# A new order of second-layer matmuls, and D parts made beside them, in a kernel of gated linear attention and four-expert layers

## Chip, cores, metric

One core of a Trainium2 chip. The metric is the device time of one execution, in microseconds (us), lower is better. Executions of one kernel agree within some 0.3%; all runs quoted are marked fast on record.

## The reference, cut

```python
# attention: B=4, H=8, S=768, D=48, state per head
for t in range(S):
    state = alpha[:, :, t, :, None] * state + k[:, :, t] (x) v[:, :, t]
    y[:, :, t] = q[:, :, t] @ state
x = y as (3072, 384)
# four experts, all used: w1 is (4, 384, 1024), w2 is (4, 1024, 384)
p = domain_probs / (domain_probs.sum(-1, keepdims=True) + 1e-9)
for e in range(4):
    out += p[:, e:e+1] * (maximum(x @ w1[e], 0) @ w2[e])
```

## The kernel before

The 3072 rows are 24 blocks of 128, in groups: 0 has two blocks, 1 to 5 have four each, 6 has two. For each group and expert a first layer makes eight hidden tiles (128 features x up to 512 rows), and a second layer multiplies them with w2. From group 2 on the operands of the second layer are in three parts: H (top), L (rest), D (a small correction of the two). H and L products share one sum per block, D has another. There are 16 second layers of full groups (96 matmuls each) and four of group 6 (48). Attention for later groups runs in between.

The first layer makes H on ScalarE, L on VectorE, then half of D at once; the other half goes on a list:

```python
def hidden_parts(x, parts):
    top, low, dif = parts
    nc.scalar.activation(out=top, in_=x, func=ACT.Relu, scale=TRIM)
    yield
    nc.vector.scalar_tensor_tensor(out=low, in0=x, scalar=0.0, in1=top.bitcast(F32),
                                   op0=ALU.max, op1=ALU.subtract)
    n = x.shape[-1]
    at = n // 2 if n == NT else 0
    if at:
        make_dif(*(part[:, :at] for part in parts))
    later.append([part[:, at:] for part in parts])
```

The second layer takes two blocks per call, all their H and L and then all their D. It allots its sums at the start of the call, from the same four buffers (tag "g") that the first layer's sums use:

```python
sums = [[ps.tile([P, DM], F32, name=f"ops{j}", tag="g", bufs=4)
         for j in range(2 if halves_ else 1)] for _ in slots]
kinds = [((0, 1), range(FCH - 2)), ((0, 1), range(FCH - 2, FCH)), ((2,), range(FCH))]
...
    if later and n % 4 == 3:
        make_dif(*later.popleft())
    ... nc.tensor.matmul(sums[i][part // 2], lhsT=h[:, part], rhs=w, ...)
    if part >= 1 and fc == FCH - 1:
        add_up(gi, e, slots[i], part // 2, ...)     # mostly one VectorE operation
```

The last second layer before a new group also splits that group's input (`split_x`, tile xT), in steps at 0, 52, 62 and 72% of the layer.

## Time and profile before

| | before |
|---|---|
| time, 3 runs | 1073.79 us (1073.01 to 1075.13) |
| span in the profile | 1071.6 us |
| TensorE busy | 98% |
| VectorE busy | 72%, 775.2 us |
| second-layer matmuls waiting for add-ups | 4.3 us, four times |

In the profile's lines PE is TensorE, PEld its weight loads, DVE VectorE, ACT ScalarE and POOL GpSimd. An instruction has its line of code, engine, output<-inputs, shapes and count; a wait has its total in us, how often it came, and the longest. The granted clock is the share of the full TensorE clock that the profile shows, as a mean over the span. The chain is the work that ended last, followed back to the start. Busy TensorE isn't the same as TensorE at full pace, so I also read distances from one matmul's start to the next. The prediction below shows the lines.

### The profile page before, as it was taken

The numbers are of one execution on the slowest core, as the hardware profiler recorded it, in microseconds if no ns is written. First come the engines' busy times: TensorE is split into PE (matmuls) and PEld (weight loads), VectorE is DVE, ScalarE is ACT, GpSimd is POOL, SyncE is SP. The second block draws the span as 40 slices with busy tenths as digits, with TensorE's granted clock in tenths as the row PEclk, the third lists the DMA queues.
The fourth block names the chain that finished last, engine by engine and source line by source line (L and its number), as shares of the span: only waits on it lengthen the run. The fifth ranks groups of instructions, "written<-read, shape, count | busy, mean of one in ns | idle before, by whom it ended". The sixth has DMA issues, their size and how long they took to land.

```text
span 1071.6 us, 21614 instructions
## 1 busy us (share of the span) xinstructions
PE 1048.1 (98%) x8460; PEld 899.1 (84%) x8460; DVE 775.2 (72%) x1711; ACT 566.7 (53%) x1202; POOL 32.7 (3%) x71
## 2 busy tenths in 40 slices
PE   8899999999999999999999999999999999999998
PEld 8777777676776798898898898898889889898988
DVE  5488776656566978778877777986787866666565
ACT  5687866575656554536546445555464543323232
POOL 2010000000000100000000000000000000000000
PEclk9999999999999999999999999999999999999999
DMA  8597699687696967758759558586594543544540
GB/s 123 156 330 216 230 328 368 238 328 241 236 309 209 402 216 274 281 160 312 268 170 359 204 187 337 186 281 234 158 358 173 221 192 147 207 177 178 187 181 31
DMA packets 158838, 251.67 MB, mean 235 GB/s; under 512 B 120112, under 2 KB 135344, under 8 KB 136208
## 3 DMA queue, kind: packets, MB, share of 16 engines
q1 hardware_dynamic: 149600, 208.82, 57.1%
q0 software_dynamic: 5760, 41.29, 9.8%
q8 instruction: 67, 1.10, 0.4%
q10 hardware_dynamic: 3376, 0.17, 0.3%
q14 instruction: 35, 0.29, 0.1%
HBM read 207.79 MB, written 42.47 MB: 234 GB/s over the span
## 4 chain that ended last, share of the span: by engine, by line
PE 83%; DVE 8%; ACT 6%; issue 2%; DMA 1%; SPq 0%; DVEq 0%; ACTq 0%
PE ops L624 25%; PE one L540 21%; PE ops L628 10%; PE two L540 10%; PE sc L334 6%; PE yps L428 3%; PE tp L266 3%; PE one L532 2%; ACT qb L308 2%; PE far L389 1%; PE sps L463 1%; DVE near L344 1%; DVE t L553 1%; DVE hT L580 1%; DVE hT L590 1%
## 5 line engine op out<-in xcount | busy, mean ns | idle before, releaser
L624 PE MATMUL ops<-w,hT 128*128 128x384 f32 x1728 | 318.0, 339 | 4.4 <-DVE acc L658 4.3
L624 PEld LDWEIGHTS ops<-w,hT 128*128 128x128 f32 x1728 | 299.1, 188 | 9.9 <-DVE acc L658 5.6
L540 PE MATMUL one<-xT,w 128*128 128x512 f32 x960 | 253.8, 400 | 2.6 <-DVE xT L248 1.1
L540 PEld LDWEIGHTS one<-xT,w 128*128 128x128 f32 x960 | 176.3, 188 | 41.8 <-DVE QT L315 1.6
L551 ACT ACTIVATE t<-one 128x512 f32<-128x512 f32 (+1 forms) x192 | 106.3, 554 | 153.6 <-PE one L540 148.5
L308 ACT COPY qb<-QT 64x256 f32<-64x256 f32 x336 | 136.4, 406 | 77.0 <-DVE QT L289 44.1
L578 ACT ACTIVATE hT<-t 128x512 fp32r<-128x512 f32 (+1 forms) x160 | 94.3, 589 | 123.6 <-DVE t L553 122.9
L580 DVE SCALAR_TENSOR_TENSOR hT<-t,hT 128x512 fp32r<-128x512 f32 (+1 forms) x160 | 102.2, 638 | 55.7 <-ACT hT L578 53.6
L540 PE MATMUL two<-xT,w 128*128 128x512 f32 x480 | 136.7, 393 | 0.0
L628 PE MATMUL ops<-hT 128*128 128x384 f32 x384 | 133.4, 491 | 0.0
L553 DVE TENSOR_TENSOR t<-t,two 128x512 f32<-128x512 f32 (+1 forms) x160 | 100.8, 630 | 41.9 <-ACT t L551 21.4
L590 DVE SCALAR_TENSOR_TENSOR hT<-hT 128x256 fp32r<-128x256 f32 x288 | 111.9, 422 | 4.4
L540 PEld LDWEIGHTS two<-xT,w 128*128 128x128 f32 x480 | 90.6, 189 | 20.0
L628 PEld LDWEIGHTS ops<-hT 128*128 128x128 f32 x384 | 69.5, 190 | 40.1 <-issue 0.4
L315 DVE TENSOR_TENSOR QT<-QT,dec 128x256 f32<-128x256 f32 x144 | 60.8, 422 | 38.2 <-ACT qb L308 37.5
L344 DVE COPY_PREDICATED near<-masks,sc 128x256 f32<-128x256 uint8 x144 | 77.0, 535 | 15.5 <-PE sc L334 12.8
L334 PEld LDWEIGHTS sc<-qb,KT 128*64 128x64 f32 x2304 | 72.7, 138 | 9.7 <-issue 5.6
L334 PE MATMUL sc<-qb,KT 128*64 128x64 f32 x2304 | 77.2, 223 | 2.6 <-ACT qb L308 2.6
L658 DVE SCALAR_TENSOR_TENSOR acc<-ops,p_all,acc 128x384 f32<-128x384 f32 x82 | 49.5, 614 | 33.9 <-PE ops L624 14.5
L326 ACT COPY KT<-KT 128x256 f32<-128x256 f32 x144 | 59.9, 416 | 3.2
L327 DVE TENSOR_TENSOR KT<-KT,dec 128x256 f32<-128x256 f32 x144 | 60.3, 419 | 0.0
L558 DVE TENSOR_TENSOR hT<-t,two 128x512 f32<-128x512 f32 x32 | 22.0, 688 | 35.6 <-ACT t L551 23.0
(88 smaller groups left out, 970.7 us busy)
## 6 DMA issues: line engine op xcount, KB each, us to landing
w<-kept SPq DMA_DIRECT2D x144, 1152.0 KB
kept<-w POOLq DMA_DIRECT2D x32, 1152.0 KB, 7.4
hT<-in_moe_w_dram SPq DMA_DIRECT2D x32, 384.0 KB
w<-in_moe_w_dram SPq DMA_DIRECT2D x48, 128.0 KB
ra<-in_alpha_dram SPq DMA_DIRECT2D x23, 192.0 KB
rk<-in_k_dram SPq DMA_DIRECT2D x23, 192.0 KB
rq<-in_q_dram SPq DMA_DIRECT2D x23, 192.0 KB
out_dram<-acc POOLq DMA_DIRECT2D x18, 192.0 KB, 6.6
```

The source lines that it names most:

```text
L308: nc.scalar.copy(out=qb[rows, :, i, :].rearrange("p a (b r) -> p a b r", r=m), in_=qv[rows])
L315: nc.vector.tensor_mul(qv, qv, spread(dv[:, :, :, 0], m))
L334: nc.tensor.matmul(out[HALF * s:HALF * (s + 1), 2 * p:2 * p + 2, :], lhsT=KTs[li][:, p, HALF * s:HALF * (s + 1)], rhs=qbs[li][:, p, :, QUA ...
L344: nc.vector.copy_predicated(near.rearrange("p a (b two r) -> p a b two r", two=2, r=m)[:, :, :, 1, :], mk.unsqueeze(1).broadcast_to([P, H, ...
L540: nc.tensor.matmul(out, lhsT=w[:, part, kc], rhs=x_part(gi, part, kc), start=(part == terms[0] and kc == 0), stop=(part == terms[-1] and k ...
L551: nc.scalar.activation(out=t, in_=one, func=ACT.Copy, scale=FINE)
L553: nc.vector.tensor_add(t, t, two)
L578: nc.scalar.activation(out=top, in_=x, func=ACT.Relu, scale=TRIM)
L580: nc.vector.scalar_tensor_tensor(out=low, in0=x, scalar=0.0, in1=top.bitcast(F32), op0=ALU.max, op1=ALU.subtract)
L590: nc.vector.scalar_tensor_tensor(out=dif, in0=top.bitcast(F32), scalar=1 / 4096.0, in1=low.bitcast(F32), op0=ALU.mult, op1=ALU.subtract)
L624: nc.tensor.matmul(sums[i][part // 2], lhsT=h[:, part], rhs=w, start=(fc == 0 and part != 1), stop=(fc == FCH - 1 and part != 0))
L628: nc.tensor.matmul(sums[i][0], lhsT=h[:, 2].bitcast(F32), rhs=w, start=(fc == 0), stop=(fc == FCH - 1))
```

## The change

The second layer takes all four blocks in one call: H and L of blocks 0 and 1, H and L of blocks 2 and 3, then D of all. A sum is allotted when its first matmul comes. D parts are no longer made in the first layer but one whole tile at a time beside the second. The input splits move to 0, 60, 70, 78%. The diff, cut to its core:

```diff
-        n = x.shape[-1]
-        at = n // 2 if n == NT else 0
-        if at:
-            make_dif(*(part[:, :at] for part in parts))
-        later.append([part[:, at:] for part in parts])
+        later.append(parts)
...
-        sums = [[ps.tile(...) for j in range(2 if halves_ else 1)] for _ in slots]
-        kinds = [((0, 1), range(FCH - 2)), ((0, 1), range(FCH - 2, FCH)), ((2,), range(FCH))]
+        pairs = [slots[k:k + 2] for k in range(0, len(slots), 2)]
+        sides = [[((0, 1), in_parts[:-2]), ((0, 1), in_parts[-2:])], [((3,), whole), ((2,), in_parts)]]
+        steps = [(side, slot, part, fc) for side in range(2) for pair in pairs
+                 for parts, tiles in sides[side] for part in parts for slot in pair for fc in tiles]
...
-            if later and n % 4 == 3:
+            if later and n % (len(steps) // 12 - 1) == len(steps) // 12 - 2:
                 make_dif(*later.popleft())
+            at = (side, slot)
+            if n == begins[at]:
+                sums[at] = ps.tile([P, DM], F32, name="ops", tag="g", bufs=4)
...
-            each = 2 if split2(gi, e) else 1
+            each = len(groups[gi]) if split2(gi, e) else 1
...
-                    for step, at in enumerate((0.0, 0.52, 0.62, 0.72)):
+                    for step, at in enumerate((0.0, 0.6, 0.7, 0.78)):
```

More of the change, by code (lines that the diff above doesn't have):

```diff
@@ L154 @@
     split1 = lambda gi, e: gi > 0
-    split2 = lambda gi, e: gi > 1
+    split2 = lambda gi, e, c=0: gi > 1
     makes = [lambda gi, e: gi == 0, lambda gi, e: gi == 1]
@@ L551, in up @@
             nc.scalar.activation(out=t, in_=one, func=ACT.Copy, scale=FINE)
-            if split2(gi, e):
+            if split2(gi, e, c):
                 nc.vector.tensor_add(t, t, two)
@@ L600, in down @@
         first = first_piece(gi, e)
-        halves_ = split2(gi, e)
+        in_parts = [fc for fc in range(FCH) if split2(gi, e, fc // FPQ)]
+        whole = [fc for fc in range(FCH) if fc not in in_parts]
         if slots[0] == 0 and makes[1](gi, e):
-            making.extend(split_piece(1, first + k) for k in range(NQ))
+            making.extend(split_piece(1, first + k) for k in range(NQ) if not split2(gi, e, k))
         if slots[0] == 0 and makes[0](gi, e) and 0 < e < E - 1:
             making.extend(split_piece(0, first + k) for k in range(2, NQ))
-        sums = [[ps.tile([P, DM], F32, name=f"ops{j}", tag="g", bufs=4)
-                 for j in range(2 if halves_ else 1)] for _ in slots]
@@ L609, in down @@
-        kinds = [((0, 1), range(FCH - 2)), ((0, 1), range(FCH - 2, FCH)), ((2,), range(FCH))]
-        steps = [(part, i, fc) for parts, tiles in (kinds if halves_ else [((3,), range(FCH))])
-                 for part in parts for i in range(len(slots)) for fc in tiles]
-        for n, (part, i, fc) in enumerate(steps):
+        pairs = [slots[k:k + 2] for k in range(0, len(slots), 2)]
+        sides = [[((0, 1), in_parts[:-2]), ((0, 1), in_parts[-2:])], [((3,), whole), ((2,), in_parts)]]
+        steps = [(side, slot, part, fc) for side in range(2) for pair in pairs
+                 for parts, tiles in sides[side] for part in parts for slot in pair for fc in tiles]
@@ L613, in down @@
+        begins = {key: n for n, key in reversed([*enumerate(step[:2] for step in steps)])}
+        ends = {step[:2]: n for n, step in enumerate(steps)}
+        sums = {}
+        for n, (side, slot, part, fc) in enumerate(steps):
             c, f = divmod(fc, FPQ)
-            h = hidden[c][:, :, f, slots[i] * P:(slots[i] + 1) * P]
-            advance(cost(1, gi, e) / FCH / (3 if halves_ else 1))
+            advance(cost(1, gi, e) * len(slots) / len(steps))
             while between and n >= between[0][0] * len(steps):
@@ L617, in down @@
                 between.popleft()[1]()
-            if n == len(steps) // 2:
+            if n and n % (len(steps) // (2 * len(slots))) == 0:
                 background()
-            if later and n % 4 == 3:
+            if later and n % (len(steps) // 12 - 1) == len(steps) // 12 - 2:
                 make_dif(*later.popleft())
-            if halves_:
+            at = (side, slot)
+            if n == begins[at]:
+                sums[at] = ps.tile([P, DM], F32, name="ops", tag="g", bufs=4)
@@ L623, in down @@
+            h = hidden[c][:, :, f, slot * P:(slot + 1) * P]
+            if part < 3:
                 w = wt[1][first + c].rearrange("p t (c d) -> p t c d", d=DM)[:, part, f]
-                nc.tensor.matmul(sums[i][part // 2], lhsT=h[:, part], rhs=w,
-                                 start=(fc == 0 and part != 1), stop=(fc == FCH - 1 and part != 0))
+                h = h[:, part]
             else:
                 w = wt[1][first + c].rearrange("p (c d) -> p c d", d=DM)[:, f]
-                nc.tensor.matmul(sums[i][0], lhsT=h[:, 2].bitcast(F32), rhs=w,
-                                 start=(fc == 0), stop=(fc == FCH - 1))
@@ L630, in down @@
-            if part >= 1 and fc == FCH - 1:
-                add_up(gi, e, slots[i], part // 2, sums[i][part // 2 if halves_ else 0])
+                h = h[:, 2].bitcast(F32)
+            nc.tensor.matmul(sums[at], lhsT=h, rhs=w, start=(n == begins[at]), stop=(n == ends[at]))
+            if n == ends[at]:
+                add_up(gi, e, slot, side, sums.pop(at))
         while between:
```

## The prediction

> **What bounds the kernel now.** I read the page's head first, then its digits, then the table of stretches of 100 us.
>
> ```profile
> span 1071.6 us, 21614 instructions
> PE 1048.1 (98%) x8460; PEld 899.1 (84%) x8460; DVE 775.2 (72%) x1711; ACT 566.7 (53%) x1202; POOL 32.7 (3%) x71
> ...
> PE   8899999999999999999999999999999999999998
> ...
> PE 83%; DVE 8%; ACT 6%; issue 2%; DMA 1%; SPq 0%; DVEq 0%; ACTq 0%
> ```
>
> TensorE is busy all along, and 83% of the chain that ended last is its work. It was idle for 1071.6 - 1048.1 = 23.5 us. Where is that idle time?
>
> ```profile
> 0.00:100.00 100.00, 89.04 (x931) 74.19 (x932) 65.36 (x159) 70.90 (x163) 9.26 (x27) 1.00 0.75 198
> 100.00:200.00 100.00, 96.42 (x911) 73.83 (x910) 70.15 (x150) 69.20 (x149) 6.39 (x12) 0.98 0.89 305
> ...
> 1000.00:1072.00 72.00, 67.67 (x403) 63.24 (x401) 43.39 (x96) 21.76 (x48) 0.00 (x0) 1.00 0.39 148
> ```
>
> The columns after the stretch are TensorE, weight loads, VectorE and ScalarE busy. 11.0 us of idle lie in the first 100 us and 3.6 in the second, while the first two groups of blocks run; their layers are not in parts, so the change does not touch them. 4.3 us are the tail (last sum, last store). That leaves 23.5 - 14.6 - 4.3 = 4.6 us in the middle 800 us, where the changed code runs. TensorE's waits name them (total us, times, longest):
>
> ```profile
> PE ops L624 <- DVE acc L658: 4.3, 4, 1.9
> ...
> PE one L540 <- ACT t L551: 0.5, 1, 0.5
> ```
>
> So second-layer matmuls waited four times for an add-up by VectorE. The timeline shows how, in one of the four:
>
> ```profile
> 754.62 8.64 PE L624 MATMUL ops<-w,hT 128*128 128x384 f32 x48
> 765.17 2.35 PE L624 MATMUL ops<-w,hT 128*128 128x384 f32 x12 [1.90 <-DVE acc L658]
> ...
> 761.92 1.43 DVE L590 SCALAR_TENSOR_TENSOR hT<-hT 128x256 fp32r<-128x256 f32 x4
> ...
> 764.50 0.61 DVE L658 SCALAR_TENSOR_TENSOR acc<-ops,p_fine,acc 128x384 f32<-128x384 f32 x1
> ```
>
> A pass over one pair of blocks is 48 matmuls: 32 for H and L, 16 for D. After exactly 48 the next pair wants the sum buffer of the first block's H and L, whose add-up began only at 764.50: VectorE was late with D parts (L590) and attention. The other three are at 593.30, 677.00 and 851.84, also after 48 matmuls. From start to start the four gaps are 0.81, 0.83, 2.24 and 1.77 us where a normal step is 0.174, so they cost 0.64 + 0.66 + 2.07 + 1.60 = **5.0 us**.
>
> Why is VectorE late? In the first layer of a full group (8 tiles of 512 columns), with no attention around:
>
> ```profile
> 918.34 0.69 DVE L580 SCALAR_TENSOR_TENSOR hT<-t,hT 128x512 fp32r<-128x512 f32 x1 [0.70 <-ACT hT L578]
> 919.07 0.42 DVE L590 SCALAR_TENSOR_TENSOR hT<-hT 128x256 fp32r<-128x256 f32 x1
> 919.41 0.68 DVE L553 TENSOR_TENSOR t<-t,two 128x512 f32<-128x512 f32 x1
> 920.79 0.69 DVE L580 SCALAR_TENSOR_TENSOR hT<-t,hT 128x512 fp32r<-128x512 f32 x1 [0.70 <-ACT hT L578]
> ...
> 914.62 1.54 PE L540 MATMUL one<-xT,w 128*128 128x512 f32 x6
> 916.00 0.85 PE L540 MATMUL two<-xT,w 128*128 128x512 f32 x3
> 916.68 1.53 PE L540 MATMUL one<-xT,w 128*128 128x512 f32 x6
> ```
>
> A tile takes TensorE 916.68 - 914.62 = 2.06 us, and the loop VectorE add, ScalarE H, VectorE L, VectorE half of D takes 920.79 - 918.34 = 2.45 us. VectorE and ScalarE fall behind 0.39 us per tile, up to 3 us per layer; the four sum buffers hide it from TensorE, but the second layer begins with that debt.
>
> **What the Trainium skill says.** "Perfetto Trace Analysis", Identifying Performance Opportunities: a repeating gap on the engine that should be saturated can mean that there is not enough PSUM for the next tile. This trace agrees: the gap is always at step 48, on a sum buffer. "VectorE: DVE Perf Modes", The TRN2 errata, gives an fp32 two-tensor operation of N columns (N+151)/0.96 ns and says that a large tile pays the fixed part once. That is 424 ns for 256 and 691 for 512; the trace has 422 (L590) and 680 to 690 (L553, L580). "TensorE: Matmul & The Clock Gate", Wait — 56ns, gives N/2.4 + 2.5 ns from start to start: 162 ns for 384 columns, 216 for 512. The trace has 174 and 229 as usual steps in undisturbed layers (96 matmuls from 880.40 to 897.16), some 7% above. So what lies outside waits is close to the floor, and only waits can be won.
>
> **The change part by part.** Matmuls: the same number, shapes and weights, in another order (32 H and L for blocks 0 and 1, 32 for 2 and 3, then 16 and 16 for D). 1728 steps of 174 ns before and after: **0**. The order view of the two kernels confirms equal counts; it only shows attention's pieces falling at slightly other places.
>
> Buffers: before, the third pair of buffers was wanted at step 48, with the first H and L sum complete at about step 30, so VectorE had some 18 steps, 3.1 us. After, blocks 2 and 3 begin at step 32 in buffers which the first layer's evictions have freed; the first D sum comes at step 64, 34 steps (5.9 us) after its predecessor was complete; the third at step 80, some 18 steps after the H and L sum of block 2 (complete near 62). The first slack nearly doubles; the other stays at 3.1 us but comes after VectorE has had 62 steps to catch up. I count the 5.0 us as gone.
>
> D parts: L590 had 288 instructions, 256 of them in full groups (16 expert passes x 8 tiles x 2 halves); those become 128 of 512 columns. In a row, six halves took 2.10 us, so one takes (2.10 - 0.42)/5 = 0.336 us; a 512-column one follows its forerunner after 0.61 us (L248 to L249 spacing without a wait). 2 x 0.336 - 0.61 = 0.06 us per tile. Those made in the first layer also waited for L (0.73 us after its start instead of 0.61), so 0.12 us more. 128 x 0.18 = **23 us of VectorE work saved**, all off the path: 2% of the span on an engine that isn't the bound.
>
> First-layer loop: without the half of D the loop is shorter by 919.41 - 918.34 - 0.61 = 0.46 us, so 1.99 us against TensorE's 2.06. The debt no longer grows. That also removes the 0.48 us wait at 833.64, the small delays after step 6 (intervals of 307, 330 and 306 ns in the last full-group layers, 438 in one: 0.7 us over 174 in all). Gain **1.2 us**.
>
> Second layer: eight whole D parts (4.9 us) instead of eight halves (2.7 us), spread over steps 6 to 55 instead of 3 to 31. The last D part is issued at step 55 and read at step 71: 16 steps, 2.8 us of slack. The splits of the next group's input move from 52/62/72% to 60/70/78% of the last second layer before a group; the last is issued 21 steps (3.7 us) before the next layer. Three such places lie among attention and D-stage VectorE work at some 90%: I allow **+1.0 us** for lateness there and at D.
>
> Sum: 1073.8 - 5.0 - 1.2 + 1.0 = **1068.6 us**, 0.5% less.
>
> **The rivals.** (a) The wait moves instead of going: VectorE has 2.2 us more to do in each second layer, so D matmuls (step 64 on) or buffers at step 80 wait. For: VectorE is busy 85 to 95% in the second layers with most attention, and its add-up there came 4 to 5 us late. Against: that lateness came from first-layer debt and from D crowded into the first 32 steps. If it holds at the four places with 1 us each, 1072 to 1073. (b) The three input splits come too late for the next group's first matmuls. For: such a wait stands in the trace at 167.22 (1.13 us, on xT L248). Against: where a group begins later, the last split ended 1.9 us before. If late by 1 to 1.5 us at three places: about 1072. (c) VectorE is a hidden bound among attention, and 23 us less of it pulls more forward. Against: outside the listed waits matmuls keep 174 and 229 ns. All idle of the middle is 4.6 us; with small delays, a floor near 1066. (d) The clock: the page's second stretch has a granted clock of 0.98 after two waits at the first group change; with the splits moved, that could go or double, about 1.7 us either way.
>
> **Range and chances.** The floor of (c) with luck in (d) is 1065; (a) and (b) together give 1074. Eight in ten: 1065.5 to 1072.5. 2% would be 21 us: to win it, the change would have to remove more than all waits outside start and tail; to lose it, it would need a new wait of over 1 us in each of the 20 second layers. Faster 0.01, within 2% 0.98, slower 0.01.
>
> **What would show it.** Right: no wait of second-layer matmuls for acc; 160 D-part instructions, 128 of them near 690 ns; VectorE's busy time down by some 20 us with TensorE's idle in the middle 800 us under 1.5 us; a first-layer loop of about 2.06 us on VectorE, no longer 2.45. Wrong: waits of second-layer matmuls for D parts or for acc at steps 64 to 80, or of first-layer ones for xT. If the waits vanish and the time doesn't fall, the four gaps were not on the path that sets the end.

## The result

| | before | after |
|---|---|---|
| time, 4 runs each | 1074.46 us (1073.01 to 1075.27) | 1067.55 us (1067.20 to 1068.25) |
| ratio, 95% interval | | 0.9938 (0.9921 to 0.9955) |
| span in the profile | 1071.6 us | 1065.4 us |

A ratio is the mean time of one kernel's fast runs over that of the other's of the same rounds, so not quite the ratio of the medians. The change is a clear gain of 0.6%, and within 2% as foreseen.

The head of the page after, and its chain:

```profile
span 1065.4 us, 21479 instructions
PE 1046.1 (98%) x8460; PEld 900.1 (84%) x8460; DVE 762.0 (72%) x1583; ACT 569.2 (53%) x1202; POOL 32.7 (3%) x71
...
PE 88%; ACT 5%; DVE 4%; issue 1%; DMA 1%; SPq 0%; ACTq 0%; DVEq 0%
```

VectorE's share of the chain halved, from 8 to 4%. Alone this says little: f3b below, as fast, has 8% again. TensorE's waits after no longer hold any of second-layer matmuls (L631); of first-layer ones they have:

```profile
PE one L540 <- DVE xT L248: 1.5, 2, 0.8
...
PE one L540 <- DMA w<-kept: 1.1, 1, 1.1
...
PE one L540 <- ACT t L551: 0.4, 1, 0.4
```

The same second layer as in the prediction, in the timeline after. 60 matmuls run on past step 48 without a gap, then attention, then the other 36:

```profile
753.28 10.76 PE L631 MATMUL ops<-w,hT 128*128 128x384 f32 x60
...
767.65 6.51 PE L631 MATMUL ops<-w,hT 128*128 128x384 f32 x36
774.00 1.54 PE L540 MATMUL one<-xT,w 128*128 128x512 f32 x6
```

From its first matmul to the first of the next layer it took 777.47 - 754.62 = 22.85 us before and 774.00 - 753.28 = 20.72 now. Measured so, the four layers with gaps lost 0.61, 0.77, 2.13 and 1.70 us: 5.2 in all. The loop of the first layer without attention, VectorE after:

```profile
913.36 0.69 DVE L580 SCALAR_TENSOR_TENSOR hT<-t,hT 128x512 fp32r<-128x512 f32 x1 [0.70 <-ACT hT L578]
914.04 0.69 DVE L553 TENSOR_TENSOR t<-t,two 128x512 f32<-128x512 f32 x1
915.42 0.69 DVE L580 SCALAR_TENSOR_TENSOR hT<-t,hT 128x512 fp32r<-128x512 f32 x1 [0.70 <-ACT hT L578]
```

915.42 - 913.36 = 2.06 us, TensorE's own pace, where it was 2.45. The D parts as groups, first of the kernel before, then after:

```profile
L590 DVE SCALAR_TENSOR_TENSOR hT<-hT 128x256 fp32r<-128x256 f32 x288 | 111.9, 422 | 4.4
```

```profile
L586 DVE SCALAR_TENSOR_TENSOR hT<-hT 128x512 fp32r<-128x512 f32 (+1 forms) x160 | 93.1, 632 | 0.0
```

And one new wait. Where the first layers of group 2 begin, after group 1, the timeline after has this on TensorE and VectorE:

```profile
352.14 0.93 PE L540 MATMUL one<-xT,w 128*128 128x512 f32 x2
353.76 1.21 PE L540 MATMUL one<-xT,w 128*128 128x512 f32 x4 [0.69 <-DVE xT L248]
...
352.15 0.96 DVE L230 TENSOR_TENSOR w<-w 128x768 fp32r<-128x768 f32 x1
353.02 0.69 DVE L248 TENSOR_TENSOR xT<-x_raw,xT 128x512 fp32r<-128x512 f32 x1
```

The third matmul waits for the last split of xT, which now stands behind a weight split (L230). That layer took 22.40 us before and 23.37 now.

### The profile page after: what moved, and what is told of

Same layout as the page of the kernel before. It is cut to its first block, busy times and chain, and to the rows that moved or that the text cites. A ratio compares the mean times of both kernels' runs of the same rounds, so it can differ in the third digit from the quotient of the medians.

```text
span 1065.4 us, 21479 instructions
## 1 busy us (share of the span) xinstructions
PE 1046.1 (98%) x8460; PEld 900.1 (84%) x8460; DVE 762.0 (72%) x1583; ACT 569.2 (53%) x1202; POOL 32.7 (3%) x71
## 4 chain that ended last, share of the span: by engine, by line
PE 88%; ACT 5%; DVE 4%; issue 1%; DMA 1%; SPq 0%; ACTq 0%; DVEq 0%
PE ops L631 37%; PE one L540 23%; PE two L540 11%; PE sc L334 6%; PE yps L428 3%; PE tp L266 3%; PE one L532 2%; ACT qb L308 2%; PE sps L463 1%; PE far L389 1%; DVE w L228 1%; DMA rv<-in_v_dram 1%; DVE near L344 1%; DMA rq<-in_q_dram 1%; ACT KT L326 1%
## 5 line engine op out<-in xcount | busy, mean ns | idle before, releaser
L631 PE MATMUL ops<-w,hT 128*128 128x384 f32 x1728 | 315.4, 339 | 0.0
L631 PEld LDWEIGHTS ops<-w,hT 128*128 128x128 f32 x1728 | 299.5, 188 | 2.5 <-ACT t L551 0.6
L631 PE MATMUL ops<-hT 128*128 128x384 f32 x384 | 133.4, 491 | 0.0
L631 PEld LDWEIGHTS ops<-hT 128*128 128x128 f32 x384 | 69.6, 190 | 39.9 <-issue 0.7
L586 DVE SCALAR_TENSOR_TENSOR hT<-hT 128x512 fp32r<-128x512 f32 (+1 forms) x160 | 93.1, 632 | 0.0
```

The source lines that it names most:

```text
L586: nc.vector.scalar_tensor_tensor(out=dif, in0=top.bitcast(F32), scalar=1 / 4096.0, in1=low.bitcast(F32), op0=ALU.mult, op1=ALU.subtract)
L631: nc.tensor.matmul(sums[at], lhsT=h, rhs=w, start=(n == begins[at]), stop=(n == ends[at]))
```

## The experiments

**Theory A**: the order is what pays, since it gives a sum buffer 34 steps to come free instead of 18. **Theory B**: VectorE's relief is what pays, and the order is only a frame for it. A third question is what the moved splits do. Kernels of one call ran on the same chip and share its runs of the kernel before.

### e1_order_only: order new, D parts and splits old

```diff
 # against the changed kernel
-        later.append(parts)
+        n = x.shape[-1]
+        at = n // 2 if n == NT else 0
+        if at:
+            make_dif(*(part[:, :at] for part in parts))
+        later.append([part[:, at:] for part in parts])
-            if later and n % (len(steps) // 12 - 1) == len(steps) // 12 - 2:
+            if later and n % 4 == 3:
# and the splits at 0, 52, 62, 72%
```

> The new order alone: D parts in halves of 256 columns, one half in the first layer, and the splits of the next input as in the kernel before. Theory A (the order gives a sum buffer 34 steps of slack instead of 18): the four waits of second-layer matmuls for acc are gone, about -5 us against before, 1069 to 1070; the first-layer loop on VectorE stays at 2.45 us and the small delays of step 6 stay (0.7 us). Theory B (the gain is VectorE's relief by whole D parts made beside the second layer, the order matters little): waits for acc stay at 2 us or more, time 1072 or more.

Measured: 1068.22 us, ratio 0.9950 (0.9937 to 0.9963), a little under the 1069 to 1070 expected. The waits of second-layer matmuls for acc are gone; the small delay of step 6 stays (the attention-free layers of group 5 take 17.0 to 17.1 us as before, 16.64 in the changed kernel's first trace). Theory A holds: the order alone gives most of the gain. What the other parts add, some 0.1%, is within the intervals.

By lengths of layers the order gave 4.6 of the 5.2 us. The layer with the second gap still took 20.48 us (20.60 before, 19.83 in the changed kernel): its wait for an add-up went to the first-layer matmuls behind it, and it took the later splits to remove that (e3 below).

```profile
PE one L540 <- DVE acc L664: 0.3, 1, 0.3
```

The later allotment of the sums is part of e1's order; it was not tested apart.

### e2_dparts_only: D parts whole and beside the second layer, order old

```diff
 # against the kernel before
-        if at:
-            make_dif(*(part[:, :at] for part in parts))
-        later.append([part[:, at:] for part in parts])
+        later.append(parts)
```

> Whole D parts beside the second layer, in the order of before: all eight within steps 3 to 31, as that order needs them from step 32. Theory A: 4.9 us of D parts where 2.7 were, ahead of the add-ups, so the waits at step 48 stay or grow, and D matmuls may wait from step 32; 1072 to 1080. The first-layer loop falls to about 2.06 us and the delays at step 6 go. Theory B: the waits for acc go without the new order, 1069 or less.

Measured: 1123.05 us, ratio 1.0461 (1.0445 to 1.0477), far worse than Theory A's range. Its TensorE waits, clock digits and a piece of its timeline:

```profile
PE ops L620 <- DVE hT L586: 22.8, 59, 1.6
...
PEclk9999999999999999999999989999899999999999
...
796.09 0.44 PE L620 MATMUL ops<-w,hT 128*128 128x384 f32 x1 [0.16 <-DVE hT L586]
796.69 0.44 PE L620 MATMUL ops<-w,hT 128*128 128x384 f32 x1 [0.16 <-DVE hT L586]
```

D matmuls from step 32 wait one by one for their D part: 0.60 us from start to start, of which the profile counts 0.16 as idle. Three costs add up: 22.8 us of counted waits; what each broken stretch loses besides (0.60 - 0.174 - 0.16 = 0.27 us, some 59 times, an estimate of 16 us); and a granted clock of 0.983 where it was 0.998, 1.5% of 1120 us = 17 us. Less the 4.3 us of old waits for acc, which are gone (the D matmuls wait ahead of them), that is some 51 us, against 48.7 more in the spans. So whole D parts made beside the second layer cost 49 us in the old order, and nothing that shows in the new one, which puts D last. The order isn't one of two equal parts but the condition of the other.

### e4_late_halves: order old, second halves of D made beside the second pair

```diff
 # against the kernel before
-            if later and n % 4 == 3:
+            if later and n % 4 == 3 and (slots[0] > 0 or len(groups[gi]) == 2):
```

> The kernel before in its own order, but the second halves of D (blocks 2 and 3) are made from step 51 on, beside the second pair, not in the first 32 steps: 2.7 us less VectorE work ahead of the add-up that step 48 waits for. If the add-up was late because VectorE was crowded, the four gaps of 0.64, 0.66, 2.07 and 1.60 us all but vanish (each was under 2.7 us), 1069 to 1070 without any new order. If the lateness has another cause (ScalarE, the sums themselves), they stay and the time is 1073 to 1075.

Measured: 1077.30 us, ratio 1.0033 (1.0019 to 1.0047): a miss. The waits say why:

```profile
PE ops L624 <- DVE hT L590: 4.6, 7, 2.0
...
PE ops L624 <- DVE acc L658: 1.6, 1, 1.6
...
686.42 0.77 PE L624 MATMUL ops<-w,hT 128*128 128x384 f32 x2 [2.00 <-DVE hT L590]
```

Three of four waits for acc went, so those add-ups (2.9 of the 5.0 us) had indeed been late because VectorE was crowded ahead of them. The longest stayed, 1.55 us where it was 1.90. There no D part of the second half stood ahead any more, but attention's operations did, and one of them waited for ScalarE, with VectorE idle:

```profile
766.29 0.43 DVE L315 TENSOR_TENSOR QT<-QT,dec 128x256 f32<-128x256 f32 x1 [1.49 <-ACT qb L308]
...
767.10 1.14 DVE L658 SCALAR_TENSOR_TENSOR acc<-ops,p_fine,acc 128x384 f32<-128x384 f32 x2
```

So for the largest gap crowding by D parts isn't shown to be the cause: without them, ScalarE's part of attention made the add-up nearly as late (9.5 us into the layer, 9.9 before). In e1 the same add-up comes 9.9 us into its layer again (at 761.70), and no matmul waits for it: the new order doesn't make the add-up earlier, it lets it be late. The delayed halves, for their part, made D matmuls wait at the end of the second pair (7 waits, 4.6 us). Six of the seven, the longest above among them, are in last second layers before a group, where the input splits stand in between. In neither of the two places tried in the old order is the work free: early it delays an add-up, late it delays D. I had reckoned only the first.

### e3_splits_back, f0_after_again, f1_splits_by_group, f2_splits_earlier: where the splits belong

```diff
 # e3: everywhere; f1: only while groups 0 and 1 run; f2: as f1, but 0, 40, 50, 60%
-                    for step, at in enumerate((0.0, 0.6, 0.7, 0.78)):
+                    for step, at in enumerate((0.0, 0.52, 0.62, 0.72)):
```

> The changed kernel with the splits of the next input back at 52, 62 and 72% of the last second layer. The trace after shows a new wait of first-layer matmuls for xT of 0.7 us at 352.7, where the first layers in parts follow those of group 1. If the later splits cause it, it is gone and the time is about 1 us under the changed kernel, 1066.5. If it comes from elsewhere, it stays and the time is the same, 1067.5. A third way: earlier splits stand before D parts on VectorE and make second-layer matmuls wait for D parts; then over 1068.

e3: 1067.33 us, ratio 0.9941 (0.9928 to 0.9955). The wait at the change from group 1 to 2 is gone (that first layer is back at 22.40 us), so the later splits cause it. But two last second layers before a group became longer (20.44 us against 19.83, 19.35 against 18.56). So the changed places help two group changes (from 3 to 4 and from 4 to 5, by 0.61 and 0.79 us) and hurt one (0.97 us); in sum nothing is seen. f0 is the unedited changed kernel as a control:

> The changed kernel unedited, as a control on the same chip as the next three: 1067 to 1068.5, with the 0.7 us wait for xT at the first layer after group 1, as in its first trace.

> The changed kernel with the old places of the input splits only while groups 0 and 1 run, the new ones after. With all splits back the wait for xT at 352.7 went, but two last second layers got longer (20.44 for 19.83 us, 19.35 for 18.56). If each place suits its stage, this takes the better half of both: the xT wait gone and those layers at 19.8 and 18.6, so 1 us under the control. If the two effects are only chance of one execution, it equals the control.

> As the run before, with the splits while groups 0 and 1 run earlier still (40, 50, 60%). At the change from group 0 to 1 first-layer matmuls waited 1.1 us for a weight transfer and 0.8 us for xT in the trace after. If xT is late there only because it is split late, that 0.8 us goes as well: another 0.5 to 0.8 us. If the input itself or VectorE's queue is late, the wait changes its name and the time is that of the run before.

| | time, us | ratio to before, 95% |
|---|---|---|
| f0, control | 1067.92 (1066.36 to 1068.14) | 0.9941 (0.9930 to 0.9953) |
| f1 | 1067.48 (1065.66 to 1068.98) | 0.9940 (0.9928 to 0.9953) |
| f2 | 1066.04 (1065.35 to 1067.65) | 0.9930 (0.9917 to 0.9943) |

In f0's trace the layer after group 1 took 23.37 us again, so the new wait isn't chance. In f1's it took 22.40 us and the two second layers kept 19.83 and 18.48, as expected; in the times its 1 us doesn't show. f2 is the fastest kernel: 1066.04 us, ratio 0.9930 to before. Its lead over the control is 1.9 us by medians, but the intervals overlap, so it is not shown. At the first group change its gain over f0 and f1 is some 0.4 us in the traces: the wait for xT went, and a wait of 1.6 us put down to another VectorE operation stands there.

### f3b_small_pieces: does the width of 512 columns matter?

```diff
-                make_dif(*later.popleft())
+                parts, n_ = later.popleft(), len(groups[gi]) * P
+                m = min(n_, NT // 2)
+                for k in range(0, n_, m):
+                    make_dif(*(t[:, k:k + m] for t in parts))
```

A first attempt (f3) didn't build: it sliced past the end in group 6.

> The changed kernel with each D part of a full group made as two pieces of 256 columns at the same place in the second layer (the earlier attempt did not build). My account: the width of a piece is worth 0.06 us of VectorE per tile, 8 us in all, off the path, so the time is that of the changed kernel within 1 us, 1067 to 1068.5. Rival: the width is what gives the slack; then second-layer matmuls wait for D parts and the time is over 1070.

Measured: 1067.62 us, ratio 0.9948 (0.9934 to 0.9962); VectorE busy 769.8 us against 762.0. So the width is worth 7.8 us of VectorE, as worked out (8), and nothing of the time that these runs can tell.

### g1_extra_half, g2_extra_whole: how much slack did the rival leave?

```diff
 # g1: half of each D part of a full group made again; g2: the whole
-                make_dif(*later.popleft())
+                parts = later.popleft()
+                make_dif(*parts)
+                if len(groups[gi]) == 4:
+                    make_dif(*(t[:, :NT // 2] for t in parts))
```

> The changed kernel with every D part of a full group followed by a useless repeat of its first half: 8 x 0.34 = 2.7 us more VectorE work per second layer, at the same steps. It measures how far the rival of the prediction (VectorE short of time in the second layer) was from coming true. If the new order leaves much slack: under 1069.5. If VectorE, busy about 90% there, is nearly the bound: waits for D parts or for acc of 0.5 to 1.5 us in some 10 of 16 layers, 1072 to 1082.

> The same with the whole D part repeated: 8 x 0.61 = 4.9 us more per second layer. With much slack under 1071; with VectorE as the bound there, 2 to 4 us in each of 12 layers with attention beside them, 1090 to 1115, and a lower granted clock as in the run with the old order and D parts beside.

| | time, us | ratio to before, 95% | VectorE busy, us | granted clock |
|---|---|---|---|---|
| changed kernel | 1067.55 (1067.20 to 1068.25) | 0.9938 (0.9921 to 0.9955) | 762.0 | 0.998 |
| g1 | 1094.09 (1092.57 to 1096.97) | 1.0202 (1.0183 to 1.0221) | 812.6 | 0.997 |
| g2 | 1136.58 (1131.71 to 1137.77) | 1.0580 (1.0558 to 1.0602) | 847.3 | 0.978 |

TensorE's waits, g1 first, then g2:

```profile
PE ops L634 <- DVE hT L586: 11.9, 15, 1.8
...
PE ops L634 <- DVE acc L663: 1.8, 2, 1.1
```

```profile
PE ops L634 <- DVE hT L586: 37.6, 35, 2.0
```

Both are misses: they cost more than I expected. 3.2 us more VectorE work per second layer (812.6 - 762.0 = 50.6 us over 16) cost 26 us of time, some half of it. In second layers without attention nothing changed in g1 (16.64 us each in the last three); 23 us of the loss lie in the 12 with attention beside them, 1.9 us in each. So VectorE is close to being the bound there, and the changed kernel lives on little slack. The repeats write the same D part again, so D matmuls wait for them as well: g1 and g2 test slack before D's deadline, not VectorE's time as such.

## Why the prediction was right

The time (1067.55, predicted 1068.6) is in the range, and by the right mechanism.

- **The four gaps, 5.0 us**: gone, 5.2 us by lengths of layers. e1 shows that the order does 4.6 of it. Why the add-ups were late, the prediction has in part: e4 shows the crowding by D parts for three gaps; for the largest, attention's wait for ScalarE is nearly enough.
- **Slack at steps 64 and 80**: held. No second-layer matmul waits in the changed kernel. TensorE's idle time in the middle 800 us is 1.06 us, under the 1.5 foreseen. Before it was 5.05 us by the rows of the table of stretches and not 4.6: the last row reaches 0.4 us past the span.
- **First-layer loop and small delays, 1.2 us**: the loop is at 2.06 us as foreseen (I worked out 1.99, which TensorE then holds back). Second layers without one of the gaps lost 2.1 us together, more than the 0.7 I had counted; in f0, the same kernel, it was 1.1 us, so half of that is the luck of one execution. The 0.48 us wait for ScalarE's t, which I also counted, did not go: it is 0.4 us.
- **Allowance for late splits, +1.0 us**: too small (1.5), and wrong in place. A wait of first-layer matmuls for xT was one of my signs of being wrong, and a new one came (0.69 us). I had looked at three changes among full groups in parts; the wait came at the change from group 1 to 2, which I left out because its second layers aren't in parts. That layer lost 0.97 us, and two later first layers 0.5 together. The same move gained 0.6 us in the layer of the second gap (e1, e3), which I hadn't counted.
- **VectorE saves 23 us**: it saved 13.2 (775.2 to 762.0). The step that failed is the 0.12 us per tile for the wait between L and its D half. f3b measures the width at 7.8 us, so place gave only 13.2 - 7.8 = 5.4 us, 0.04 us per tile. I had compared starts (0.73 against 0.61 us). But 0.04 of the 0.73 was idle and not busy time (918.34 + 0.69 to 919.07), and in the changed kernel's loop the next instruction follows L after 0.68 us (913.36 to 914.04), not 0.61. As VectorE was off the path, it cost nothing. The 0.61 is the distance from L249 to its follower, too; from L248 to L249 it is 0.71 (511.58 to 512.29).
- **Rival (a), VectorE short of time in the second layer**: did not come, but I thought it further away than it was. My argument was about when the work falls; g1 shows that the amount counts as well.
- **Rival (c), a floor near 1066**: doesn't follow from its figures; 1073.8 - 5.0 - 1.2 is 1067.6.
- **Rival (d), the clock**: a stretch at half clock near 167 us is in the traces before and after (clock 0.998) and missing in f0, which is the changed kernel unedited (clock 1.0). So it comes and goes by execution; none of it may be credited to the change.

## What to carry to other kernels

When the engine that should be saturated waits for a sum buffer at the same step each time, ask what stands in the queue of the engine that empties it, and whether another order of the same matmuls lets that engine be late. Place deferrable work by its own deadline as well as by what it delays: it was harmless beside a second layer only once its consumers had moved to the end (e1 and e2: -5.6 and +49 us for the two halves of one change). Then measure the slack left by adding useless work, since an engine at 72% over the whole span may be full in the stage that matters.

## What the Trainium skill lacked or had wrong

- "TensorE: Matmul & The Clock Gate", Why this matters for your kernels, sets about 3 us of TensorE idle as the gap that brings the lower clock. In e2 no single wait for a D part was over 1.6 us, yet the granted clock fell to 0.983; in g2, with none over 2.0 us, to 0.978. The same page's section on a second failure mode tells of short repeated idling, but gives no size for it.
- The same page's N/2.4 + 2.5 ns, which the prediction took for the floor, is 162 and 216 ns; here 174 and 229 are usual. The page itself, under Back-to-back issue gap, calls it the gap of an isolated matmul and gives about 131 ns for 512 columns in a stream with weight loads, which no run here comes near. No page has a second pace of the same stream at the same granted clock: two executions of the same code ran the same attention-free second layer, 96 matmuls without a wait, in 16.64 us (after) and 16.96 us (f0), both at a granted clock of 1.00. The stretches of the two kernels, with TensorE, weight loads, VectorE and ScalarE busy, then clock:

```profile
976.71:993.35 16.64, 16.64 (x98) 16.64 (x96) 10.60 (x18) 0.80 (x2) 0.00 (x0) 1.00 0.01 2
```

```profile
976.35:993.31 16.96, 16.96 (x98) 16.96 (x96) 10.59 (x18) 0.80 (x2) 0.00 (x0) 1.00 0.01 2
```

- What sets that pace stays open. It is 2% of a layer and comes and goes within one execution, so differences of 1 us between single traces mean little.
